# Linear attention and memory attention, four layers: the second multiplier of the queries behind the merge's `kt` loop, the opening's input parts behind the powers, segment 1's moments behind the keys, and a second pause in the preparation of weights

## The chip, the core and the metric

The kernel runs on one core of one Trainium2 chip. The metric is the time of one launch on the device in microseconds, less is better. The core's engines are TensorE (PE: matrix products and transposes, with weight loads counted apart as PEld), VectorE (DVE), ScalarE (ACT), GpSimd (POOL) and SyncE (SP). Each works through its own row of instructions in order; an instruction that waits holds up everything behind it on its engine. DMA transfers are issued by SP, ACT and POOL from the same rows and run beside the engines.

## The reference

The input x has 2048 rows of 640 numbers. Two kinds of layers, A and B, are applied in turn, A, B, A, B, each to the normalised x, and each adds its result to x.

```
# layer A: linear attention, 32 heads of 20
qkv = layernorm(x) @ wqkv
pq, pk = phi(q), phi(k)             # t + 1 where t > 0, else exp(t); + 1e-6
kv  = einsum("bhsd,bhse->bhde", pk, v);  z = sum over s of pk
o   = (pq @ kv) / (pq . z + 1e-6)
x   = x + o @ wo
# layer B: four segments of 512 rows; in each head
o   = g * (pq @ M) / (pq . z + 1e-6) + (1 - g) * softmax(q k^T / sqrt(20) + mask) @ v
M, z += the segment's phi(k)^T v and sum of phi(k)
x   = x + o @ wo
```

## The kernel before

**Layer A without v.** A layer A never computes v. For every segment of 512 rows (four tiles of 128) it computes the keys' features `pk` (L525 to L536) and the queries' features, which go to DRAM as `pqd` (L542, L543). Then it gathers `G`, the normalised input transposed times `pk`, over the four segments (memory matmuls, L557, added up in the tiles `v` and `g_last`, L562, L564). Only when all segments are in does `merge` form the one matrix that maps queries to results: it broadcasts the sums of `z` (`zb`, L609 to L612), scales `G` and splits it (`gs`, L625 to L628), multiplies with `w_Av` (L642) to block matrices `kt` (L647 to L654, one for each of five blocks of columns), and multiplies these with `w_Ao` to `wm` (L674, L679, L681, L682; "the product"). The queries are then read back a tile at a time by `p_read` (L698): the tile `pqi` is multiplied by `zb` on POOL (L700), summed by head on DVE and inverted (L703 to L705), and multiplied by that on POOL (L706). Then it is transposed on PE (L319) and goes through `wm` (`o_half`, L472).

**Splits.** For precision a weight or an activation is held as the sum of two f16 tensors, so most products are three matmuls. ACT makes the high half, and DVE or POOL the low one: L264 and L265 for weights, L323 and L324 for transposed inputs, L476 (ACT) and L477 (POOL) for the normalised inputs `xs` ("the input parts"), L530 and L531 for the keys, L653 and L654 for `kt`.

**The opening.** While the first layer A runs, the eight weights are prepared (`w_prep`): loaded as f32 into one of two `stage` buffers, reduced to their largest absolute value (L240 five times, L245, a PE transpose at L248, L250, a PE broadcast at L254), scaled by a power of two (L257 to L260), split (L264, L265) and stored to DRAM (`wd`, L270). Layers fetch them again later (L276, on POOL's queue). Normalising an input tile takes the moments (L338 to L345 on DVE, the power -1/2 at L343 on POOL) and one ACT instruction (L368) that makes `xh`; four PE transposes of it make `xT`.

**What sets the order.** The code is made of generators that yield the cost of the matmuls they have just written. `weave` alternates a main generator with a side one: after each step of the main one, two or three steps of the side one (`per`). `pause(n)` yields n empty steps, so it puts n main-side turns, that is their matmuls, between two parts of a side generator. PE's order is the order in which the code was written. The rows of the other engines are set by a scheduler that takes what is ready first by its estimate, and in cases of doubt what was written first. `issue_after(ins)` makes what is written inside it stand behind `ins` on the engine of `ins`. `a_head`, which calls `p_read` for the first three tiles, looks at each turn whether `L["zb"]` is set, and begins when it is. During the merge `filled` puts the last queries' steps between the parts.

Of the kernel before, what the change touches and what calls it, by code (L numbers as in the profile page):

```python
# [21 lines left out]
P = 128  # L22
# [105 lines left out]
def pause(n):  # L128
    for _ in range(n):
        yield 0.0  # L130
# [12 lines left out]
class Kernel:  # L143
# [84 lines left out]
    def w_prep(self, key, stage, w, wait=0, behind=False):  # L228
# [15 lines left out]
        m1 = cp.tile([P, 1], F32, name="wm1", tag="wm1", bufs=2)  # L244
        nc.vector.tensor_reduce(m1, mx, axis=AX.X, op=OP.max)  # L245
        yield 0.0
        pt = self.bank()
        nc.tensor.transpose(pt[:1, :P], m1, self.ident)  # L248
        m2 = cp.tile([1, 1], F32, name="wm2", tag="wm2", bufs=2)
# [83 lines left out]
    def moments(self, x):  # L333

        nc, sb = self.nc, self.sb
        st = sb.tile([P, 2, 6], F32, tag="st", name="st", bufs=3)
        for k in range(2):
            nc.vector.bn_stats(st[:, k], x[:, k * HN:(k + 1) * HN])  # L338
        mv = sb.tile([P, 2], F32, tag="mv", name="mv", bufs=4)
        nc.vector.bn_aggr(mv, st)  # L340
        rs = sb.tile([P, 1], F32, tag="rs", name="rs", bufs=4)
        self.taken = nc.vector.tensor_scalar(rs, mv[:, 1:2], 1e-5, None, op0=OP.add)
        nc.gpsimd.tensor_tensor(rs, rs, self.mhalf, op=OP.pow)  # L343
        nb = sb.tile([P, 1], F32, tag="nb", name="nb", bufs=4)
        self.last = nc.vector.tensor_scalar(nb, mv[:, 0:1], rs, -1.0, op0=OP.mult, op1=OP.mult)  # L345
        return x, nb, rs
# [135 lines left out]

    def norms(self, src, s, box, gap):

        box.append([self.moments(self.load_x(src, s, i)) for i in range(NT)])
        yield from pause(gap)
        yield from self.g_norms(s, box)

# [26 lines left out]
    def g_first(self, s, box, w, L, behind=None):  # L515
# [7 lines left out]
        def keys(i):  # L523
# [3 lines left out]
            for n in range(2):  # L527
                z, c = slice(n * HN, (n + 1) * HN), slice(n * (HN + 1), n * (HN + 1) + HN)
                e = self.phi_a(self.proj_n(xT, w("k"), i, n), self.inv["A", "k"])
                nc.scalar.activation(pk[i][:, 0, c], e, AF.Copy, scale=self.k_scl)  # L530
                nc.vector.scalar_tensor_tensor(pk[i][:, 1, c], e, self.k_scl, pk[i][:, 0, c],  # L531
                                               op0=OP.mult, op1=OP.subtract)
                if s == 0 and i == 0:
                    (nc.gpsimd if L["early"] else nc.vector).tensor_copy(L["z"][:, z], e)
                else:
                    (nc.gpsimd if L["early"] else nc.vector).tensor_tensor(L["z"][:, z], L["z"][:, z], e, op=OP.add)  # L536
                yield self.COST_N
# [50 lines left out]
    def merge(self, L, wv, wo, memory, fill):  # L588
# [26 lines left out]
        for n in range(2):  # L615
# [4 lines left out]
            for c in range(C):  # L620
# [4 lines left out]
                nc.vector.scalar_tensor_tensor(e, L["G"][c][:, n * (HN + 1):n * (HN + 1) + HN], eps[:, c:c + 1],  # L625
                                               rz[:, n * HN:(n + 1) * HN], op0=OP.add, op1=OP.mult)
                nc.scalar.activation(t[:, c, 0, :HN], e, AF.Copy)
                L["split"] = nc.vector.tensor_tensor(t[:, c, 1, :HN], e, t[:, c, 0, :HN], op=OP.subtract)  # L628
        L["zb"] = zb
        for _ in memory:  # L630
            pass
        yield from filled(1)
# [1 line left out]
        for t in range(C):  # L634
# [16 lines left out]
                                           self.blk[:, OFF[t]:OFF[t] + WID[t]].rearrange(h, e=E1)[:, :, :DH],  # L651
                                           op0=OP.mult, op1=OP.mult)
            nc.scalar.activation(k2[:, 0, P:P + hi - lo], e, AF.Copy)  # L653
            nc.vector.tensor_tensor(k2[:, 1, P:P + hi - lo], e, k2[:, 0, P:P + hi - lo], op=OP.subtract)  # L654
            kt.append(k2)
            yield 15 * (hi - lo) * COL
            if t == 1:
                yield from filled(1)
        for v in L["v"]:
            self.ones_column(v)  # L660
        wm = sb.tile([P, C, 2, D], F16, tag="wo", name="wm", bufs=2)
# [405 lines left out]
    def opening(self, src, stage, L, box):  # L1067
# [46 lines left out]
        m = [m]  # L1114
        with self.tc.issue_after(self.last.ins):
            m += [self.moments(x[i]) for i in range(2, NT)]
        def others():
            xh = [first]
            for i in range(1, NT):
                xh.append(self.normed(*m[i - 1]))  # L1120
                yield from self.turn(xh[i], cur[1], i)
            for i in range(NT):
                self.parts(xh[i], cur[2], i)

        o = others()
        self.ones_columns()
# [155 lines left out]
```

## Time and profile before

| | us |
|---|---|
| median of 3 runs | 1739.72 (1735.49 to 1740.57) |
| profiled execution | 1736.56 |
| its span, first to last instruction | 1734.8 |
| mean granted PE clock | 0.992 |
| PE busy | 1651.8 (95%) |
| DVE busy | 1252.2 (72%) |
| ACT busy | 995.6 (57%) |
| POOL busy | 541.1 (31%) |

A row of the time line reads: start in us, duration in us, engine, line, operation, tile written <- tiles read, sizes, xcount (equal instructions in succession are one row), and in brackets how long the engine sat idle before it and what ended that wait. A PE row of many matmuls runs to the start of the next one when there is no bracket. A clock below 1 in the tables means that the matmuls of that stretch ran slower by a throttle. The chain on the page has PE at 70%, DVE at 13%, ACT at 7%: an engine that is busy is not by that on the path.

### The profile page before, as it was taken

To read this page: it belongs to the slowest core of one execution; us is meant where nothing else is said; L and a number is where in the kernel's file an instruction comes from. 1 tells how busy PE (TensorE), PEld (TensorE's weight loads), DVE (VectorE), ACT (ScalarE), POOL (GpSimd) and SP (SyncE) were. 2 spreads that over 40 slices of the span, in tenths; PEclk is the share of its full clock that TensorE was granted. 3 is DMA by queue.
4 is the path that set the end of the run, shared out by engine and by line. 5 is a ranking of instruction groups with operands and counts; after the bars stand their busy time and mean duration, and the time that the engine had idled before them with its cause. 6 is when DMAs were issued, how large, how long until landed. Compare 5 with 4: busy or idle time off the path is not lost.

```text
span 1734.8 us, 36293 instructions
## 1 busy us (share of the span) xinstructions
PE 1651.8 (95%) x13032; PEld 1031.2 (59%) x13032; DVE 1252.2 (72%) x3966; ACT 995.6 (57%) x1883; POOL 541.1 (31%) x1059
## 2 busy tenths in 40 slices
PE   6999989999999999999999999999999999999998
PEld 4677656564465456556566777666546545645555
DVE  7878696387787768768874466846778877878773
ACT  5666433346747646667776554333675576666673
POOL 3542132123213433433452310221422432332452
PEclk9999999999999999999999999999999999999999
DMA  5424563332222331353211303523232323223432
GB/s 214 148 99 147 205 231 125 114 104 70 99 86 60 111 115 65 123 164 112 70 55 39 115 31 115 179 97 121 67 105 83 113 79 110 99 81 112 133 113 92
DMA packets 110365, 190.89 MB, mean 110 GB/s; under 512 B 14172, under 2 KB 69596, under 8 KB 107624
## 3 DMA queue, kind: packets, MB, share of 16 engines
q1 hardware_dynamic: 97704, 142.68, 25.3%
q0 software_dynamic: 3264, 24.91, 4.1%
q10 hardware_dynamic: 9216, 20.98, 3.1%
q8 instruction: 103, 1.69, 0.4%
q14 instruction: 78, 0.64, 0.1%
HBM read 109.32 MB, written 78.64 MB: 108 GB/s over the span
## 4 chain that ended last, share of the span: by engine, by line
PE 70%; DVE 13%; ACT 7%; DMA 4%; issue 3%; POOL 2%; SPq 1%; ACTq 0%; POOLq 0%; DVEq 0%
PE ps L395 28%; PE ps L381 13%; PE ps L993 7%; PE ps L557 4%; PE ps L966 4%; PE ps L925 3%; PE ps L319 3%; ACT pe L970 3%; PE ps L446 2%; DVE ps L931 2%; PE ps L810 2%; PE ps L1006 1%; DVE xn L472 1%; DVE split L265 1%; DVE st L338 1%
## 5 line engine op out<-in xcount | busy, mean ns | idle before, releaser
L931 DVE CUSTOM_DVE_ANT_0 ps<-ps,maskw 128x384 f32<-128x384 f32 (+3 forms) x1024 | 472.9, 519 | 37.2 <-PE ps L925 34.2
L970 ACT ACTIVATE pe<-ps,lsc 128x512 f32<-128x512 f32 x640 | 396.3, 698 | 76.3 <-PE ps L966 74.4
L395 PEld LDWEIGHTS <-xT 128*128 128x128 f16 x2880 | 282.4, 99 | 115.8 <-issue 8.6
L977 POOL TENSOR_SCALAR_AFFINE_SELECT pe<-pe 128x256 f32<-128x256 f32 (+1 forms) x640 | 230.2, 367 | 369.1 <-ACT pe L970 362.4
L395 PEld LDWEIGHTS <-oT 128*128 128x128 f16 x1920 | 184.5, 98 | 81.6 <-issue 5.9
L993 PE MATMUL ps<-pe,v 128*32 128x512 f32 (+3 forms) x2048 | 165.7, 439 | 12.6 <-POOL pe L977 7.3
L931 DVE DVE_READ_ACCUMULATOR2_ANT mg<- 128x1 f32 x1024 | 143.7, 140 | 0.0
L395 PE MATMUL ps<-w_Ak,xT 128*128 128x320 f16 x960 | 141.1, 304 | 2.7 <-ACT w_Ak L264 1.5
L395 PE MATMUL ps<-wm,oT 128*128 128x320 f16 x960 | 141.7, 299 | 2.0
L381 PE MATMUL ps<-xT,w_Bq 128*128 128x512 f16 x600 | 140.3, 379 | 2.8 <-ACT r L419 1.6
L395 PE MATMUL ps<-w_Bo,oT 128*128 128x320 f16 x960 | 141.2, 299 | 1.5 <-ACT oT L323 0.7
L395 PE MATMUL ps<-w_Aq,xT 128*128 128x320 f16 x960 | 140.5, 303 | 1.2 <-DVE xT L324 1.1
L557 PE MATMUL ps<-pk,xs 128*128 128x321 f16 (+1 forms) x960 | 139.0, 302 | 2.1 <-DVE pk L531 1.4
L395 PE MATMUL ps<-w_Bv,xT 128*128 128x320 f16 x960 | 139.7, 299 | 0.6 <-DVE otok L1013 0.6
L381 PE MATMUL ps<-xT,w_Bk 128*128 128x512 f16 x600 | 138.3, 379 | 1.2 <-ACT pe L970 1.2
L925 PE MATMUL ps<-ks,qs 60*128 60x512 f16 (+3 forms) x1024 | 122.9, 298 | 6.8 <-ACT pe L970 3.3
L557 PEld LDWEIGHTS <-xs 128*128 128x128 f16 x960 | 93.6, 98 | 40.6 <-issue 2.1
L775 DVE SCALAR_TENSOR_TENSOR nat<-ps,nat 128x512 f16<-128x512 f32 x80 | 55.2, 690 | 82.9 <-ACT nat L774 82.8
L993 PEld LDWEIGHTS ps<-pe,v 128*32 128x32 f32 x2048 | 65.9, 110 | 74.8 <-issue 39.9
L966 PE MATMUL ps<-qs,ks 62*128 62x512 f16 (+3 forms) x1024 | 106.3, 300 | 2.3 <-ACT pe L970 1.1
L410 DVE SCALAR_TENSOR_TENSOR e<-e,r 128x320 f32<-128x320 f32 x128 | 65.2, 509 | 53.2 <-ACT r L409 52.3
L774 ACT ACTIVATE nat<-ps 128x512 f16<-128x512 f32 x80 | 48.3, 604 | 88.4 <-PE ps L381 69.6
(197 smaller groups left out, 2421.2 us busy)
## 6 DMA issues: line engine op xcount, KB each, us to landing
x<-xn ACTq DMA_DIRECT2D x48, 320.0 KB
qs<-qd SPq DMA_DIRECT2D x128, 120.0 KB
ks<-kd SPq DMA_DIRECT2D x128, 120.0 KB
xo<-x SPq DMA_DIRECT2D x48, 320.0 KB
pqi<-pqd SPq DMA_DIRECT2D x32, 320.0 KB
qd<-nat SPq DMA_DIRECT2D x40, 256.0 KB
kd<-nat SPq DMA_DIRECT2D x40, 256.0 KB
x<-in_A_x SPq DMA_DIRECT2D x16, 320.0 KB
```

Source lines behind the costliest of these rows:

```text
L319: nc.tensor.transpose(pt[:, (c - c0) * P:(c - c0 + 1) * P], src[:, c * P:(c + 1) * P], self.ident)
L381: nc.tensor.matmul(p, w[:, c, a, t * P:(t + 1) * P], xT[:, c, b, :], start=k == 0, stop=k == 3 * C - 1)
L395: nc.tensor.matmul(p, xT[:, c, a, i * P:(i + 1) * P], w[:, c, b, n * HN:(n + 1) * HN], start=k == 0, stop=k == 3 * C - 1)
L410: nc.vector.scalar_tensor_tensor(e, e, 1.0, r, op0=OP.min, op1=OP.add)
L557: nc.tensor.matmul(p, xs[:, i, a, c * P:(c + 1) * P], pk[i][:, b, cols], start=k == 0, stop=k == 3 * NT - 1)
L775: nc.vector.scalar_tensor_tensor(nat[:, 1], p, QK_SHIFT, nat[:, 0], op0=OP.mult, op1=OP.subtract)
L925: nc.tensor.matmul(bs[par][:, a:a + n], qs[r, p, i * P:(i + 1) * P], ks[r, p, :n], start=True, stop=True)
L931: nc.vector.tensor_tensor_reduce(bs[par][:, a:a + n], bs[par][:, a:a + n], self.maskw[:, SEG - n:], 1.0, NEG, OP.add, OP.max, G["mg"][:, p ...
L966: nc.tensor.matmul(b[:, a:a + n], ks[r, p, j * P:(j + 1) * P], qs[r, p, j * P:], start=True, stop=True)
L970: nc.scalar.activation(e, b, AF.Exp, scale=self.lsc)
L977: nc.gpsimd.affine_select(d, d, pattern=pat, compare_op=OP.is_ge, fill=0.0, base=0, channel_multiplier=-1)
L993: nc.tensor.matmul(G["pv"][32 * h4:32 * h4 + 32, j * P:], v[j][:, h * E1:h * E1 + 32], G.pop((p, par, j)), start=j == 0, stop=j == 2, skip ...
```

## The change

Five edits. (1) In `opening`, the input parts of segment 0 (L476, L477) are put behind the last power L343 of segment 0. The mark is a POOL instruction, so it orders POOL's L477 alone. (2) In `norms`, all loads of a segment's input are written first, and for segment 1 the moments are put behind `keyed`, the last split L531 of the keys written so far, which is a DVE instruction. (3) `w_prep` has a second `pause(wait)`, in front of the transpose of the maximum; `wait` is 0 for A's k and q, 3 for A's v and o and for B's v, q and k, and 6 for B's o. (4) In `merge`, `L["zb"]` is set behind the `kt` loop, so that `a_head` begins there. (5) `L["split"]`, behind which `p_read` writes its product L700, becomes the low split of `kt` instead of the low split of `G`.

```
@@ w_prep
         nc.vector.tensor_reduce(m1, mx, axis=AX.X, op=OP.max)
         yield 0.0
+        yield from pause(wait)
         pt = self.bank()
         nc.tensor.transpose(pt[:1, :P], m1, self.ident)
@@ moments
-        nc.gpsimd.tensor_tensor(rs, rs, self.mhalf, op=OP.pow)
+        self.power = nc.gpsimd.tensor_tensor(rs, rs, self.mhalf, op=OP.pow)
@@ norms
-        box.append([self.moments(self.load_x(src, s, i)) for i in range(NT)])
+        x = [self.load_x(src, s, i) for i in range(NT)]
+        with self.tc.issue_after(self.keyed.ins) if s == 1 else nullcontext():
+            box.append([self.moments(t) for t in x])
@@ g_first, keys
-                nc.vector.scalar_tensor_tensor(pk[i][:, 1, c], e, self.k_scl, pk[i][:, 0, c],
+                self.keyed = nc.vector.scalar_tensor_tensor(pk[i][:, 1, c], e, self.k_scl, pk[i][:, 0, c],
@@ merge
-                L["split"] = nc.vector.tensor_tensor(t[:, c, 1, :HN], e, t[:, c, 0, :HN], op=OP.subtract)
-        L["zb"] = zb
+                nc.vector.tensor_tensor(t[:, c, 1, :HN], e, t[:, c, 0, :HN], op=OP.subtract)
...
-            nc.vector.tensor_tensor(k2[:, 1, P:P + hi - lo], e, k2[:, 0, P:P + hi - lo], op=OP.subtract)
+            L["split"] = nc.vector.tensor_tensor(k2[:, 1, P:P + hi - lo], e, k2[:, 0, P:P + hi - lo], op=OP.subtract)
             kt.append(k2)
             yield 15 * (hi - lo) * COL
             if t == 1:
                 yield from filled(1)
+        L["zb"] = zb
@@ opening
+        top = self.power
...
-            for i in range(NT):
-                self.parts(xh[i], cur[2], i)
+            with self.tc.issue_after(top.ins):
+                for i in range(NT):
+                    self.parts(xh[i], cur[2], i)
```

Lines of the changed kernel are 1 higher from L248 and 2 to 3 higher from L486 (L250 is L251, L531 is L534, L654 is L656, L700 is L703, L703 is L706, L706 is L709). In the rows below a row gives line, operation, tile written <- tiles read, size and count.

On DVE near 200 us, at the maximum of `B_wk` (L250, `wm`) and the reductions of `B_wo` (L240, `wmx`), before:

```order
L531 SCALAR_TENSOR_TENSOR pk<-e,k_scl,pk 128x320
L240 TENSOR_REDUCE wmx<-stage 128x1
L410 SCALAR_TENSOR_TENSOR e<-e,r 128x320
L240 TENSOR_REDUCE wmx<-stage 128x1
L542 TENSOR_SCALAR e<-e 128x320
L250 TENSOR_REDUCE wm_2496<-ps 1x1
```

and now:

```order
L545 TENSOR_SCALAR e<-e 128x320
L251 TENSOR_REDUCE wm_2523<-ps 1x1
L411 SCALAR_TENSOR_TENSOR e<-e,r 128x320
L240 TENSOR_REDUCE wmx<-stage 128x1
L534 SCALAR_TENSOR_TENSOR pk<-e,k_scl,pk 128x320
L240 TENSOR_REDUCE wmx<-stage 128x1
```

The maximum of `B_wk` stands ahead of the first reduction of `B_wo` now, and a keys' split behind it.

On DVE in the first merge, at the first block of `kt`, before:

```order
L703 TENSOR_REDUCE rca<-pqi 128x32
L628 TENSOR_TENSOR xT<-ge,xT 128x320 x2
L410 SCALAR_TENSOR_TENSOR e<-e,r 128x320
L704 TENSOR_SCALAR rca<-rca 128x32
L703 TENSOR_REDUCE rca<-pqi 128x32
L542 TENSOR_SCALAR e<-e 128x320
L705 RECIPROCAL rca<-rca 128x32
L704 TENSOR_SCALAR rca<-rca 128x32
L647 MEMSET kt 128x512
L705 RECIPROCAL rca<-rca 128x32
L650 SCALAR_TENSOR_TENSOR ke<-ps,blk 128x140
```

and now:

```order
L649 MEMSET kt 128x512
L631 TENSOR_TENSOR xT<-ge,xT 128x320 x2
L411 SCALAR_TENSOR_TENSOR e<-e,r 128x320
L652 SCALAR_TENSOR_TENSOR ke<-ps,blk 128x140
L545 TENSOR_SCALAR e<-e 128x320
L649 MEMSET kt 128x512
L656 TENSOR_TENSOR kt<-ke,kt 128x140
```

The sums of the queries and their inverses are gone from there. They stand behind the fourth of the ten splits L685 of the product now (L682 before).

On POOL in the second merge, where `w_B...` are the fetches for the next layer, L194 writes the ones into the tiles `v`, and L700 and L706 are the two products on a queries' tile, before:

```order
L700 TENSOR_TENSOR pqi<-pqi,zb 128x640
L194 MEMSET v_83 128x32
L194 MEMSET v_84 128x32
L194 MEMSET v_85 128x32
L194 MEMSET v_86 128x32
L276 DMA w_Bv<-wd_Bv 128x6400
L706 TENSOR_TENSOR pqi<-pqi,rca 128x640
L700 TENSOR_TENSOR pqi<-pqi,zb 128x640 x2
L276 DMA w_Bq<-wd_Bq 128x6400
L706 TENSOR_TENSOR pqi<-pqi,rca 128x640 x2
L276 DMA w_Bk<-wd_Bk 128x6400
```

and now:

```order
L194 MEMSET v_83 128x32
L194 MEMSET v_84 128x32
L194 MEMSET v_85 128x32
L194 MEMSET v_86 128x32
L277 DMA w_Bv<-wd_Bv 128x6400
L277 DMA w_Bq<-wd_Bq 128x6400
L703 TENSOR_TENSOR pqi<-pqi,zb 128x640 x3
L277 DMA w_Bk<-wd_Bk 128x6400
L709 TENSOR_TENSOR pqi<-pqi,rca 128x640 x3
```

All three first products stand behind the fetches of `w_Bv` and `w_Bq`, and all three second products behind that of `w_Bk`. In the first merge the row of POOL now is `w_Bv`, `w_Bq`, the first product three times, the second once, `w_Bk`, the second twice; before, two first products stood at its head and two of the second ones ahead of `w_Bk`, with the third just ahead of it.

Elsewhere: on SP in the first merge the loads of `pqi` stand behind the store of `w_Bo` and six small stores `ks<-one` (L768), where two of them stood ahead of both. On DVE there, the five splits L265 of `w_Bo` stand behind the first splits of `G` instead of ahead of them. In the opening, POOL runs the last two powers and one copy before the first two parts, and ACT has the five high halves of `w_Aq` (L264) ahead of segment 1's first `xh` (L368), where three `xh` stood ahead of them before. PE's own order changes at the weights' transposes and broadcasts alone.

More of the change, by code (lines that the diff above doesn't have):

```diff
@@ L530, in keys @@
                 nc.scalar.activation(pk[i][:, 0, c], e, AF.Copy, scale=self.k_scl)
-                nc.vector.scalar_tensor_tensor(pk[i][:, 1, c], e, self.k_scl, pk[i][:, 0, c],
-                                               op0=OP.mult, op1=OP.subtract)
+                self.keyed = nc.vector.scalar_tensor_tensor(pk[i][:, 1, c], e, self.k_scl, pk[i][:, 0, c],
+                                                            op0=OP.mult, op1=OP.subtract)
                 if s == 0 and i == 0:
```

## The prediction, made before the changed kernel was run

> **What bounds the kernel now.** I read the page's first lines, then the list of waits of TensorE (PE), then the time line of each engine around the longest of these waits, then tables of busy time over two stretches.
>
> ```profile
> span 1734.8 us, 36293 instructions
> PE 1651.8 (95%) x13032; PEld 1031.2 (59%) x13032; DVE 1252.2 (72%) x3966; ACT 995.6 (57%) x1883; POOL 541.1 (31%) x1059
> ```
>
> PE is busy for 1651.8 of 1734.8 us, so all that an edit of order can win lies in 83 us of PE idling, and in stretches in which PE runs at a lower clock after idling.
>
> ```profile
> PE ps L319 <- ACT xh L368: 11.2, 2, 7.6
> PE ps L254 <- DVE wm L250: 4.6, 2, 4.2
> PE ps L674 <- DVE kt L654: 4.4, 2, 3.7
> ```
>
> Columns: total us, number, longest. Of the first, 7.6 us is the kernel's start, which no edit touches; the other 3.6 and the next two rows are the places of the change: the opening, the maximum of `B_wk`, and the merges. The first merge begins near 223 us, the second near 1085 us. Work elsewhere on PE keeps its order.
>
> **Edit 1: the opening's input parts behind the powers.**
>
> ```profile
> 17.84 3.21 POOL L477 TENSOR_TENSOR xs<-xh,xs 128x640 f16<-128x640 f32 x2 [2.83 <-ACT xs L476]
> ```
> ```profile
> 20.00 0.14 DVE L342 TENSOR_SCALAR rs<-mv 128x1 f32<-128x1 f32 x1
> ```
> ```profile
> 23.06 0.90 PE L319 MATMUL ps<-ident,xh 128*128 128x128 f32 x3 [3.60 <-ACT xh L368]
> 23.75 4.21 PE L395 MATMUL ps<-w_Ak,xT 128*128 128x320 f16 x15
> ```
>
> The third input's variance is ready at 20.14, but its power stands behind two parts on POOL until 21.05. With the powers first, 0.9 us of the 3.60 us wait goes. The parts (3.21 us) then run from about 22.5 us; nothing needs them before the memory matmuls at 43 us.
>
> **Edit 2: segment 1's moments behind the last split of segment 0's keys.**
>
> ```profile
> 43.41 0.30 PE L557 MATMUL ps<-pk,xs 128*128 128x321 f16 x1 [0.73 <-ACT pk L530]
> 45.10 0.43 PE L557 MATMUL ps<-pk,xs 128*128 128x321 f16 x2 [1.39 <-DVE pk L531]
> ...
> 45.79 8.35 PE L557 MATMUL ps<-pk,xs 128*128 128x321 f16 x48
> 53.98 0.71 PE L319 MATMUL ps<-ident,xh 128*128 128x128 f32 x5
> ```
> ```profile
> 49.83 3.71 ACT L264 ACTIVATE w_Aq<-stage,scl_Aq 128x640 f16<-128x640 f32 x5 [0.77 <-DVE rs L342]
> ```
>
> Without the moments ahead of them on DVE, the keys come sooner: of 0.73 and 1.39 us I take 1.4, the longer wait; with edit 1, PE comes to the transposes of segment 1 (53.98) at least 1.4 + 0.9 = 2.3 us earlier. But the order on ACT has the normalised first input of segment 1 behind the five `w_Aq` splits now, where three stood ahead of them before. Those splits end at 49.83 + 3.71 = 53.54; they may begin up to 2 us earlier with the earlier keys, and 0.9 us of normalising follows them. So the input is there at about 53.3 and PE waits for it: 0.3 us is kept of 2.3. Ends: -2 (the splits a full 2 us earlier) and +2.5 (splits not earlier, and the clock lost). Term: **-0.3**. Late next: that input.
>
> **Edit 3: one more pause in the weights' preparation.** It moves the transpose of a weight's maximum, and the broadcast behind it, 30 to 37 matmuls back on PE, for A's v and o and B's weights.
>
> ```profile
> 200.64 0.82 DVE L240 TENSOR_REDUCE wmx<-stage 128x1 f32<-128x640 f32 x1 [6.10 <-DMA stage<-in_B_wo]
> ```
> ```profile
> 203.06 0.58 PE L254 MATMUL ps<-wm,ones 1*128 1x1 f32 x2 [4.22 <-DVE wm L250]
> 203.57 7.15 PE L395 MATMUL ps<-w_Aq,xT 128*128 128x320 f16 x30
> ...
> 214.77 4.10 PE L395 MATMUL ps<-w_Ak,xT 128*128 128x320 f16 x29
> ```
>
> Before, L250 of `B_wk` stands on DVE behind a reduction that waits for `B_wo` to land, and PE waits for L250: 4.22 us, and 30 matmuls in 7.15 us where 29 take 4.10 elsewhere, so 2.9 us more by a slow clock. Now L250 stands ahead of that reduction, so the 7.1 us go. But DVE still waits at 200.64 for `B_wo`, now with a keys' split behind it:
>
> ```profile
> 222.44 0.73 DVE L531 SCALAR_TENSOR_TENSOR pk<-e,k_scl,pk 128x320 f16<-128x320 f32 x1 [0.64 <-ACT pk L530]
> ```
> ```profile
> 200.64:223.17 22.53, 20.11 (x126) 13.72 (x126) 19.04 (x38) 13.56 (x27) 7.89 (x11) 0.85 0.43 156
> 223.17:254.65 31.48, 27.88 (x247) 20.47 (x245) 30.53 (x70) 11.18 (x23) 6.65 (x10) 1.00 0.51 191
> ```
>
> (Columns: length, then busy time of PE, weight loads, DVE, ACT, POOL, then clock, DMA share, GB/s.) From that landing to the last keys' split DVE is busy 19.04 of 22.53 us. By the new order three L410, two L542 and one L250 fewer stand in between, about 2.4 us by my estimate from such rows (0.5, 0.3 and 0.3 us each). That leaves 16.6 us of work, and about 1.9 us of waits for ACT at the end (three of 0.64): the last split ends near 219, against 223.17. PE, 7 us earlier, waits for it. Ends: -7.1 (DVE does not bind) and -1 (its slack of 3.5 us not used, and the landing 0.5 to 1.6 us later, because stage buffers come free later). Term: **-4.3**. Late next: DVE, which is full from there on (30.53 of 31.48 us).
>
> **Edit 4: p_read after the `kt` loop.** The product L700 is on POOL and the marked instruction on DVE; the order shows no hold of one on the other. What moves p_read is that `zb` is published later: the loads `pqi`, L700 and the rows L703 to L706 all stand later on SP, POOL and DVE.
>
> ```profile
> 249.93 0.81 DVE L703 TENSOR_REDUCE rca<-pqi 128x32 f32<-128x640 f32 x1
> ...
> 252.90 0.34 DVE L705 RECIPROCAL rca<-rca 128x32 f32<-128x32 f32 x1
> ...
> 254.65 4.01 DVE L654 TENSOR_TENSOR kt<-ke,kt 128x140 f16<-128x140 f32 x1
> ...
> 259.33 0.23 DVE L654 TENSOR_TENSOR kt<-ke,kt 128x140 f16<-128x140 f32 x1
> ```
> ```profile
> 255.72 1.28 POOL L706 TENSOR_TENSOR pqi<-pqi,rca 128x640 f32<-128x640 f32 x1
> 256.95 1.53 POOL L700 TENSOR_TENSOR pqi<-pqi,zb 128x640 f32<-128x640 f32 x1
> ...
> 271.89 0.58 POOL L276 DMA_DIRECT2D w_Bk<-wd_Bk  x1 [4.70 <-PE ps L679]
> ```
> ```profile
> 258.71 0.45 PE L674 MATMUL ps<-w_Ak,kt 128*128 128x320 f16 x1 [3.67 <-DVE kt L654]
> 259.27 0.98 PE L679 MATMUL ps<-w_Ak,kt 128*32 128x320 f16 x3
> ...
> 264.48 0.58 PE L679 MATMUL ps<-w_Ak,kt 128*32 128x320 f16 x6
> ...
> 271.52 1.09 PE L319 MATMUL ps<-ident,pqi 128*128 128x128 f32 x8
> 272.65 2.53 PE L395 MATMUL ps<-wm,oT 128*128 128x320 f16 x15
> ```
>
> First merge. Ahead of the first `kt` split, two each of L703, L704 and L705 leave DVE: 2 x (0.81 + 0.34) = 2.3, and with the two small L704 between them I take 2.5 off the chain. The split took 4.01 us against 0.23 while POOL ran L706 and L700, and PE waited 3.67 us. With POOL's products behind it this goes, but three L700 now run back to back (4.6 us) and can hold a later split; PE then has groups of the product in hand. I take half: 1.9. Behind that wait five groups run at 0.98 us, where later ones take 0.58: 5 x 0.4 = 2 us of slow clock, of which half again, 1.0. Against that, POOL's `w_Bk` fetch waits for the last L679, and the second and third L706 stand behind it, where before they stood ahead: 0.58 + 1.28 us after the last L679 for PE's eight transposes, 0.4 us for the wake-ups between them by my estimate, and some for loads that land late, in all 2.5. Sum: -2.5 - 1.9 - 1.0 + 2.5 = **-2.9**. Ends: -7.4 (everything but 1.5 kept) and +2 (a split still held, the transposes 5 us late).
>
> The SBUF page of the Trainium skill ("SBUF — State Buffer", "Who interferes with whom") says that VectorE and GpSimd share one port pair, that the first to start holds it for its whole instruction, and that the other is blocked until then. Taken by the letter a `kt` split would wait for one product, 1.5 us, and the term would be 1 us better; the row of 4.01 us spans the whole of one L706 and one L700 with a fetch before them, so the train counts, and the sum goes by the row.
>
> Second merge:
>
> ```profile
> 1100.71 0.31 PE L674 MATMUL ps<-w_Ak,kt 128*128 128x320 f16 x1 [0.74 <-DVE kt L654]
> ...
> 1108.23 0.31 PE L679 MATMUL ps<-w_Ak,kt 128*32 128x320 f16 x1 [2.19 <-DVE kt L654]
> 1108.47 0.58 PE L674 MATMUL ps<-w_Ak,kt 128*128 128x320 f16 x3
> ```
>
> These 2.9 us go, as L703 leaves the `kt` chain. But now all three L706 stand behind `w_Bk`, so behind the last L679: 0.4 + 0.58 + 2 x 1.28 = 3.5 us of lateness, less 0.1 that overlap. Term: **+0.5**, ends -1.5 (only one product late) and +3.5 (the loads behind the fetches as well).
>
> **Sum.** -0.3 - 4.3 - 2.9 + 0.5 = -7.0. The profiled execution took 1736.56 us, so 1729.6 for one like it. It lies 3.2 us under the median of the three runs, 1739.72, whose own spread is 5 us; a median of the changed kernel should be about 1739.72 - 7.0 = 1732.7.
>
> **The rivals.** What a measurement tells from no change here is about 0.3%, 5.2 us: under 1734.5 is faster, over 1744.9 slower.
>
> A, the backlog keeps it. DVE is full from 200 to 255 us, and if the landing of `B_wo` is later by 1.6 us and the `w_Bo` splits sit in DVE's chain, edit 3 gives -1 and edit 4 its -2.9: with the others -3.7, 1736.0. For it: 30.53 of 31.48 us. Against it: the wait of 6.10 us on DVE shows that work can be put ahead.
>
> B, slower: the loads of `pqi` become the end of both merges.
>
> ```profile
> 216.01 1.40 SPq L698 DMA_DIRECT2D pqi<-pqd  x2
> ...
> 239.33 4.55 SPq L768 DMA_DIRECT2D ks<-one  x6
> ```
> ```profile
> w_Bv<-wd_Bv POOLq DMA_DIRECT2D x1, 1600.0 KB, 9.0
> ```
>
> Before, two of the first three loads were issued at 216.01; now all four stand behind the `w_Bo` store and six `ks` issues (4.55 us), beside fetches of 1600 KB that take 9.0 us. Issued at 249 (my estimate: 4.55 us and a store behind the `w_Bo` splits) and landing 8 us later, three L700 (4.6), L703 to L705 (2.5), one L706, the fetch and two more L706 (4.4 together) bring the transposes to 268.5 instead of 271.52. That is -3.0 for the edits up to there, whatever they won before it, +3.5 in the second merge, +0.5 together: 1740.2. Each us that the loads land later counts twice, so from a landing 10.4 us after the issue it is slower by over 0.3%; at 11 us, 1746. Against it: 320 KB are a fifth of such a fetch.
>
> C, the change doesn't do what it says: no edge holds L700 on POOL, so it falls on a `kt` split as before. Edit 4 then gives -2.5 + 2.5 = 0, the whole -4.1: 1735.6.
>
> D, all is kept: -2 - 7.1 - 7.4 - 1.5 = -18, 1721.7.
>
> What the new waits of 2 to 3 us do to the clock is open. The row at 45.10 (0.73 and 1.39 us of idling, then 48 matmuls in 8.35 us, 0.174 each, against 4.10 / 29 = 0.141) says 1.6 us for each; the group at 1108.47 runs at full speed (0.58 us) behind 2.19 us of idling, which says nothing. I take nothing, and put 1.6 us each into the upper ends. The Trainium skill ("TensorE: Matmul & The Clock Gate", Part 1) lets the clock fall after an idle window of about 3.4 us: by that the new waits cost nothing, as the second row has it, and the first row disagrees.
>
> **Chances.** Forecast 0.45 (own range 1727 to 1735, the four ends taken by a third), A 0.14, B 0.24, C 0.10, D 0.07. Faster are D and nearly all of the forecast (0.48 after its upper edge); A, C and that edge lie within 0.3%, 0.28; B, taken with its later landings, is the slower side, 0.24. The range takes in most of B and half the way to D: 1724 to 1746.
>
> **What would show it.** Right: no wait of PE at L254 near 203 us; the last keys' split near 219; the first `kt` split at about 0.23 us; a wait at the `pqi` transposes of 1 to 3 us in both merges, with the `w_Bk` fetch ahead of it on POOL; a wait for segment 1's first input near 50 us. Wrong, if PE waits over 5 us at those transposes, if the last keys' split is still at 222, or if the opening at 64 us is off by over 2 us.

## The result and the profile after

The changed kernel takes 1730.60 us (median of 5 runs, 1728.51 to 1732.77) against 1738.55 us (median of 5, 1735.49 to 1740.57) of the kernel before. The ratio is 0.9954, with a 95% interval of 0.9938 to 0.9970: 8.0 us less, where 7.0 less had been forecast. (The 1739.72 of the forecast was the median of the first three of these five runs of before.) The profiled execution took 1731.61 us, its span is 1729.8 us, so 5.0 less than before: the pair of profiles shows 3 us less of a gain than the medians do. The page's first lines and rows of PE's list of waits:

```profile
span 1729.8 us, 36293 instructions
PE 1649.9 (95%) x13032; PEld 1032.5 (60%) x13032; DVE 1249.1 (72%) x3966; ACT 997.0 (58%) x1883; POOL 539.3 (31%) x1059
```
```profile
PE ps L320 <- ACT xh L369: 12.0, 3, 7.7
PE ps L320 <- POOL pqi L709: 9.3, 4, 7.2
...
PE ps L255 <- DVE wm L251: 1.2, 2, 0.9
```

The waits for `kt` (4.4 us for its first rows) and for the maximum of `B_wk` (4.2) are gone from the head of the list, and a wait of 9.3 us for `pqi` has come, 7.2 of it at one place. The time line of PE shows the first merge first:

```profile
215.88 3.74 PE L560 MATMUL ps<-pk,xs 128*128 128x321 f16 x24
220.67 1.31 PE L612 MATMUL ps<-z,square 128*128 128x320 f32 x4 [1.06 <-DVE square L608]
...
249.53 0.57 PE L677 MATMUL ps<-w_Ak,kt 128*128 128x320 f16 x3
...
259.97 0.58 PE L682 MATMUL ps<-w_Ak,kt 128*32 128x320 f16 x3
260.97 0.77 PE L320 MATMUL ps<-ident,pqi 128*128 128x128 f32 x5 [0.42 <-POOL pqi L709]
262.80 0.55 PE L320 MATMUL ps<-ident,pqi 128*128 128x128 f32 x3 [1.06 <-POOL pqi L709]
263.18 2.42 PE L396 MATMUL ps<-wm,oT 128*128 128x320 f16 x15
```

and then the second:

```profile
1090.38 0.57 PE L677 MATMUL ps<-w_Ak,kt 128*128 128x320 f16 x3
...
1100.13 0.58 PE L682 MATMUL ps<-w_Ak,kt 128*32 128x320 f16 x3
1107.95 2.14 PE L320 MATMUL ps<-ident,pqi 128*128 128x128 f32 x8 [7.24 <-POOL pqi L709]
1109.88 3.61 PE L396 MATMUL ps<-wm,oT 128*128 128x320 f16 x15
1113.33 0.38 PE L320 MATMUL ps<-ident,pqi 128*128 128x128 f32 x2
```

The first merge's product runs with no wait of any size and at full clock, and pays 1.5 us at the transposes of `pqi`. The second merge's product runs through too, but then PE waits 7.24 us, and afterwards its transposes take 2.14 us and its 15 matmuls 3.61, where both merges of before have 1.09 and 2.53: the clock had fallen (0.63 in a table further down). DVE and POOL in the first merge, with the last keys' split, the first and the third split of `kt`, and the three first products:

```profile
218.70 0.72 DVE L534 SCALAR_TENSOR_TENSOR pk<-e,k_scl,pk 128x320 f16<-128x320 f32 x1 [0.64 <-ACT pk L533]
...
247.52 0.23 DVE L656 TENSOR_TENSOR kt<-ke,kt 128x140 f16<-128x140 f32 x1
...
252.37 0.62 DVE L656 TENSOR_TENSOR kt<-ke,kt 128x160 f16<-128x160 f32 x1 [2.31 <-ACT kt L655]
```
```profile
251.28 4.67 POOL L703 TENSOR_TENSOR pqi<-pqi,zb 128x640 f32<-128x640 f32 x3 [0.22 <-DMA pqi<-pqd]
```

To set one execution against another I use the starts of five rows of PE in each profile: the queries of segment 0 (its first L395 after 60 us), the memory matmuls of segment 3 (the first L557 after 205 us), the first product in the first merge (L674), its first output, and, in the second merge, from its first `w_Av` matmul to the second 15 matmuls of its first output. All entries are us, from such rows, one profile each.

| profile | start to queries, segment 0 | to memory, segment 3 | to first product | to first output | second merge | span |
|---|---|---|---|---|---|---|
| before | 64.34 | 158.56 | 31.69 | 18.06 | 24.55 | 1734.8 |
| after | 66.07 | 149.81 | 33.65 | 13.65 | 29.93 | 1729.8 |
| after less before | +1.73 | -8.75 | +1.96 | -4.41 | +5.38 | -5.0 |

The first four stages lie end to end and come to -9.5 at the first output. The stretches not in the table take off 0.9 more.

### The profile page after: what moved, and what is told of

The parts are those of the page before. It is cut to its first block, busy times and chain, and to the rows that moved or that the text cites. A ratio compares the mean times of both kernels' runs of the same rounds, so it can differ in the third digit from the quotient of the medians.

```text
span 1729.8 us, 36293 instructions
## 1 busy us (share of the span) xinstructions
PE 1649.9 (95%) x13032; PEld 1032.5 (60%) x13032; DVE 1249.1 (72%) x3966; ACT 997.0 (58%) x1883; POOL 539.3 (31%) x1059
## 4 chain that ended last, share of the span: by engine, by line
PE 73%; DVE 12%; ACT 7%; POOL 3%; issue 2%; DMA 2%; SPq 0%; ACTq 0%; POOLq 0%; DVEq 0%
PE ps L396 31%; PE ps L382 13%; PE ps L996 7%; PE ps L560 5%; PE ps L320 4%; PE ps L969 4%; PE ps L928 3%; ACT pe L973 3%; DVE ps L934 2%; PE ps L447 2%; PE ps L813 2%; PE ps L1009 1%; DVE wmx L240 1%; DMA pqi<-pqd 1%; PE ps L805 1%
```

## The experiments

### Where the change's time comes from: edit 3 alone, edits 1 to 3, edits 4 and 5

Edit 3 alone is the kernel before with one line more (the names `power`, `keyed` and `top` are set too and not used):

```
         yield 0.0
+        yield from pause(wait)
         pt = self.bank()
```

> The second pause in w_prep alone. The sum on record has -4.3 for it; the profiles so far say that PE gets 8.5 us at the memory matmuls of the last segment and gives about 2 back in the first merge. Theory T5 (this edit alone is the change's whole gain): no wait near 203 us, PE 8 to 9 us nearer to the memory matmuls of segment 3 from the queries of segment 0 than before, a kt split of 2 to 4 us in the first merge, the second merge as before, median 5 to 7 us under the kernel before. Rival R5 (edits 1 and 2 are needed for it): 3 us or less.

Measured: 1731.16 us (5 runs) against 1736.89 of before beside it, ratio 0.9965 (0.9952 to 0.9978), 5.7 us less. From the queries of segment 0 to the memory matmuls of segment 3 it takes 149.80 us, 8.8 less than before, and PE has no wait near 203 us. The held `kt` split takes 2.46 us. T5 holds, but for the second merge: it takes 25.92 us, not 24.55 as before, because three groups of its product run at 0.98 us behind a wait of 2.23 us.

The second kernel has edits 1, 2 and 3, and leaves `zb` and the mark at their old places; against the changed kernel:

```
@@ merge, behind the splits of G
+                L["split"] = nc.vector.tensor_tensor(t[:, c, 1, :HN], e, t[:, c, 0, :HN], op=OP.subtract)
+        L["zb"] = zb
         for _ in memory:
...
@@ merge, behind the kt loop
-        L["zb"] = zb
```

> Edits 1 to 3 alone; zb is published where it was before. By the sum on record these three give -0.3 - 4.3 = -4.6 us. Theory T3 (the prediction's): no wait near 203 us, the last keys' split about 4 us earlier, DVE full behind it, the kt split of 4 us and the waits at 250 to 259 us of before still there, the second merge as before; median 3 to 5 us under the kernel before. Rival R3 (without the late p_read the earlier arrival is worth nothing, since the splits wait in the first merge anyway): median within 1.5 us of the kernel before.

Measured: 1731.11 us (10 runs) against 1736.94, ratio 0.9970 (0.9959 to 0.9982), 5.8 us less. Its profile has the first product of the merge at 247.60 and the first output at 265.17, 17.57 us later, about as before (18.06): a split is still held (2.88 us, and PE waits 2.55 us for it). The second merge takes 24.44 us, as before. What T3 says of the waits holds; the last keys' split comes 6.5 us earlier, not 4, and the gain is above the 3 to 5 us that it gave. R3 falls: the earlier arrival is worth its time without the late p_read.

The third kernel has edits 4 and 5 alone; against the changed kernel:

```
@@ w_prep
-        yield from pause(wait)
@@ norms
-        x = [self.load_x(src, s, i) for i in range(NT)]
-        with self.tc.issue_after(self.keyed.ins) if s == 1 else nullcontext():
-            box.append([self.moments(t) for t in x])
+        box.append([self.moments(self.load_x(src, s, i)) for i in range(NT)])
@@ opening
-            with self.tc.issue_after(top.ins):
-                for i in range(NT):
-                    self.parts(xh[i], cur[2], i)
+            for i in range(NT):
+                self.parts(xh[i], cur[2], i)
```

> Edits 4 and 5 alone. By the sum on record they give -2.9 in the first merge and +0.5 in the second. Theory T4 (the second merge is the wrong term, +4.4 instead of +0.5, and the first merge was about right): the wait near 203 us as before (4.2 us), the first product of the first merge about 3 to 6 us earlier than before against the same place at 223 us, a wait of over 6 us at the pqi transposes of the second merge, median between 1.5 us under and 2 us over the kernel before. Rival R4 (the loads land late only because the first three edits brought the merge forward): the wait at the second merge stays under 4 us and the median is 2 to 5 us under the kernel before.

Measured: 1739.34 us (10 runs) against 1736.94, ratio 1.0012 (1.0003 to 1.0021), so 2.4 us more, a little over what T4 gave. Its first product lies 29.56 us behind the memory matmuls of segment 3 instead of 31.69, so 2.1 us nearer, where T4 gave 3 to 6. On PE, DVE and POOL of this kernel:

```profile
201.67 0.58 PE L254 MATMUL ps<-wm,ones 1*128 1x1 f32 x2 [4.36 <-DVE wm L250]
...
257.60 0.31 PE L679 MATMUL ps<-w_Ak,kt 128*32 128x320 f16 x1 [3.67 <-DVE kt L653]
...
1113.65 2.14 PE L319 MATMUL ps<-ident,pqi 128*128 128x128 f32 x8 [6.52 <-POOL pqi L706]
```
```profile
253.46 4.08 DVE L653 TENSOR_TENSOR kt<-ke,kt 128x160 f16<-128x160 f32 x1 [0.93 <-ACT kt L652]
```
```profile
252.84 4.51 POOL L700 TENSOR_TENSOR pqi<-pqi,zb 128x640 f32<-128x640 f32 x3
```

R4 falls: the second merge's wait of 6.5 us comes without the first three edits. What I had as a risk in the prediction, the three L700 in a row holding a later split, is here: the third block's split, issued during the first of them, ends with the last of them, 4.08 us later, and PE waits 3.67 us, as long as before the change. So edits 4 and 5 alone move the held split from the first block to the third and pay for the second merge on top. From the memory matmuls of segment 3 to the first output it takes 48.20 us (221.06 to 269.26) against 49.75 before: 1.5 us won there, and some 5 us lost in the second merge.

In the first merge the edits help each other. From the memory matmuls of segment 3 to the first output before takes 49.75, edits 1 to 3 take 51.45, edits 4 and 5 take 48.20, and all five 47.30, 2.6 less than the two differences add up to (49.90). These are single profiles; two more kernels, which leave the first merge as it is in the changed one, take 47.00 and 47.41.

The time in all is another matter. Edit 3 gives 5.7 us, edits 1 to 3 give 5.8, and all five 8.0 in their own comparison, with intervals of 2 to 3 us each way. The 8.0 hangs on that comparison's 1738.55 for the kernel before; against the 1736.30 to 1736.94 of the later ones, 1730.60 is 5.7 to 6.3 us less. So the whole net gain can be edit 3's, and that edits 4 and 5 add to it is not shown. The profiles say why: from edits 1 to 3 to all five, the stretch from the memory matmuls to the first output gets 4.15 us shorter and the second merge 5.49 longer.

### The second merge: when p_read is early there, the loads early, the fetch behind

The first kernel publishes `zb` early in the second merge alone, and moves the mark of edit 5 back there:

```
+        if not L["early"]:
+            L["zb"] = zb
         for _ in memory:
             pass
...
-        L["zb"] = zb
+        if L["early"]:
+            L["zb"] = zb
```

> The changed kernel, but in the second merge zb is published at its old place, so that p_read is late in the first merge alone. Theory T (the second merge costs the change about 4.4 us net, because p_read is late there): PE waits about as before at the second merge (0.7, 0.3 and 2.2 us, a wait of under 0.5 us at the pqi transposes), and the median is about 1726, 4 to 5 us under the changed kernel's 1730.6. Rival R0 (what was lost there is lost for another reason, the earlier arrival colliding with the fetches of the next layer's weights): a wait of over 3 us stays at the pqi transposes, median 1729 to 1731.

Measured: 1726.95 us (4 runs) against 1736.30, ratio 0.9948 (0.9931 to 0.9964). In the profile T holds and R0 falls: the waits in the product are 0.74, 0.25 and 2.35 us, about as before, there is none at the transposes, and the second merge takes 26.23 us instead of 29.93. The time is less clear than T gave it: 1726.95 is 3.65 us under 1730.60, but by the ratios (0.9948 and 0.9954, each against its own runs of before) no difference can be told.

The second kernel leaves p_read late in both, and writes only its first three loads early in the second merge. `L["go"]` is set in `merge` where `zb` was published before, and `p_read` takes its tile from `L["pre"]` while there are any:

```
+    def p_load(self, L, s, i):
+        pq = self.row("pqi")
+        self.q_pqi.dma_start(pq, L["pqd"][s][i])
+        return pq
...
     def a_head(self, L, s, box):
+        if L["zb"] is None and not L["early"]:
+            while not L.get("go"):
+                yield 0.0
+            L["pre"] = []
+            for i in range(3):
+                L["pre"].append(self.p_load(L, s, i))
+                yield 0.0
```

> The changed kernel, but in the second merge the first three loads of pqi are written where zb was published before; the products stay late. Theory T1 (the 7.2 us wait at the pqi transposes comes from the loads landing late, beside two fetches): the first products on POOL start at the merge's beginning or at once when written, the wait falls to 2 to 3.5 us, the clock stays up, median about 1726. Rival R1 (it comes from the row of POOL, where the second products stand behind the fetch of w_Bk): the wait stays over 5 us, median about 1730.

Measured: 1721.24 us (4 runs, 1718.87 to 1721.55) against 1736.30, ratio 0.9911 (0.9896 to 0.9926). The whole wait is gone, which is more than T1 gave. The scheduler moves the first products on POOL with the loads: they start at 1069.18, 1082.45 and 1086.09 us, two of them ahead of both fetches. SP of the changed kernel, then of this one:

```profile
1064.13 26.32 SPq L546 DMA_DIRECT2D pqd<-e  x4
1090.62 2.16 SPq L701 DMA_DIRECT2D pqi<-pqd  x4
```
```profile
1041.29 22.73 SPq L546 DMA_DIRECT2D pqd<-e  x6
1064.12 1.50 SPq L700 DMA_DIRECT2D pqi<-pqd  x3
1085.80 4.13 SPq L546 DMA_DIRECT2D pqd<-e  x2
```

POOL of the changed kernel, and the DMA engines' share there (the last three columns are clock, DMA share and GB/s):

```profile
1087.94 0.53 POOL L277 DMA_DIRECT2D w_Bv<-wd_Bv  x1 [2.95 <-PE ps L396]
1090.84 0.53 POOL L277 DMA_DIRECT2D w_Bq<-wd_Bq  x1 [2.37 <-PE ps L644]
1100.12 1.53 POOL L703 TENSOR_TENSOR pqi<-pqi,zb 128x640 f32<-128x640 f32 x1 [8.76 <-DMA pqi<-pqd]
1102.35 3.02 POOL L703 TENSOR_TENSOR pqi<-pqi,zb 128x640 f32<-128x640 f32 x2 [0.70 <-DMA pqi<-pqd]
1105.31 0.59 POOL L277 DMA_DIRECT2D w_Bk<-wd_Bk  x1
1106.64 3.72 POOL L709 TENSOR_TENSOR pqi<-pqi,rca 128x640 f32<-128x640 f32 x3 [0.73 <-DVE rca L707]
```
```profile
1090.00:1100.00 10.00, 10.00 (x84) 4.39 (x81) 5.74 (x16) 4.44 (x12) 0.53 (x1) 1.00 0.96 392
1100.00:1110.00 10.00, 2.76 (x14) 1.89 (x13) 5.30 (x13) 1.41 (x4) 8.44 (x7) 0.63 0.68 246
```

SP's row is held by the last four stores of the queries until 1090.45, and behind them stand all four loads. They go out between two fetches of 1600 KB, the DMA engines are busy for 96% of the next 10 us, and the first load has landed only when POOL can begin at 1100.12, 9.5 us after its issue. With the loads ahead of the last two stores the second merge takes 20.83 us instead of 29.93, and 24.55 before the change. PE goes straight from the product into the transposes:

```profile
1097.75 0.58 PE L683 MATMUL ps<-w_Ak,kt 128*32 128x320 f16 x3
1098.26 1.09 PE L320 MATMUL ps<-ident,pqi 128*128 128x128 f32 x8
1099.39 2.53 PE L396 MATMUL ps<-wm,oT 128*128 128x320 f16 x15
```

The third kernel is the changed one with the fetch of `w_Bk` put behind the third L709 on POOL:

```
@@ p_read
-        nc.gpsimd.tensor_tensor(q3, q3, rc[:, :, None].to_broadcast([P, H, DH]), op=OP.mult)
+        x = nc.gpsimd.tensor_tensor(q3, q3, rc[:, :, None].to_broadcast([P, H, DH]), op=OP.mult)
+        if i == 2:
+            self.third = x
@@ dense
-                    wB["k"] = self.fetch(("B", "k"))
+                    with self.tc.issue_after(self.third.ins):
+                        wB["k"] = self.fetch(("B", "k"))
```

> The changed kernel, but the fetch of w_Bk stands behind the third second product L709 on POOL in both merges. Theory T1 (the loads land late): in the second merge the wait of 7.2 us falls by 0.6 us at most, in the first merge the waits of 0.4 and 1.1 us fall to about 0.5 together; median 1729 to 1730. Rival R1 (the fetch of w_Bk holds the products): the second merge's wait falls under 4 us, median about 1726.

Measured: 1729.72 us (7 runs) against 1736.30, ratio 0.9971 (0.9960 to 0.9982). The wait at the second merge is 6.32 us instead of 7.24, so R1 falls; it is shorter by a little more than T1's 0.6. In the first merge the second of the two waits goes from 1.06 to 0.46 us: there the fetch does stand in the way, by its own 0.6 us. But PE then waits about as long for the next thing, DVE's split of the transposed tile:

```profile
260.06 1.94 PE L396 MATMUL ps<-wm,oT 128*128 128x320 f16 x13 [0.64 <-DVE oT L325]
```

From the end of the product to the second 15 matmuls it takes 5.21 us here and 5.10 in the changed kernel, so nothing is won in the first merge. Lateness of the loads is the cause in the second merge: POOL waits 8.76 us for them there, and the wait goes when they come early. The place of the fetch is a small addition at most.

### The opening: without edit 2

This kernel takes back the `norms` part of the change:

```
-        x = [self.load_x(src, s, i) for i in range(NT)]
-        with self.tc.issue_after(self.keyed.ins) if s == 1 else nullcontext():
-            box.append([self.moments(t) for t in x])
+        box.append([self.moments(self.load_x(src, s, i)) for i in range(NT)])
```

> The changed kernel without edit 2 (segment 1's moments where they were before). Theory T2 (the opening lost 1.7 us because segment 1's first normalised input now comes behind the five splits of w_Aq): no wait at segment 1's first transposes, PE at the queries of segment 0 (66.1 us in the changed kernel) about 1.7 to 2.5 us earlier, and, as DVE holds the first merge up from 201 us on, at most half of it is left at the end: median 1729 to 1730. Rival R2 (the opening lost it by edit 1, the parts on POOL at 22 to 26 us): the wait of 2.0 us at those transposes goes, but PE is no earlier at the queries of segment 0.

Measured: 1729.91 us (5 runs, 1727.34 to 1732.14) against 1736.30, ratio 0.9961 (0.9948 to 0.9974); the changed kernel's own ratio is 0.9954, so no difference can be told. No wait is left at segment 1's first transposes, and PE is at the queries of segment 0 at 62.91, 3.2 us earlier, where T2 gave 1.7 to 2.5, so R2 falls. ACT and DVE of the changed kernel show where that wait comes from:

```profile
46.76 3.71 ACT L265 ACTIVATE w_Aq<-stage,scl_Aq 128x640 f16<-128x640 f32 x5 [2.95 <-DVE scl_Aq L261]
54.35 0.92 ACT L369 ACTIVATE xh<-x,nb,rs 128x640 f32<-128x640 f32 x1 [3.88 <-DVE nb L346]
```
```profile
48.96 4.01 DVE L266 SCALAR_TENSOR_TENSOR w_Aq<-stage,scl_Aq,w_Aq 128x640 f16<-128x640 f32 x5
...
53.30 0.14 DVE L343 TENSOR_SCALAR rs<-mv 128x1 f32<-128x1 f32 x1
```
```profile
55.33 0.77 PE L320 MATMUL ps<-ident,xh 128*128 128x128 f32 x5 [2.00 <-ACT xh L369]
```

ACT has its splits of `w_Aq` done at 50.47 and then waits 3.88 us. On DVE the five low splits (4.01 us) stand ahead of L343 at 53.30, from which POOL's power and DVE's `nb` (L346) follow at once. So T2 has the mechanism right, an input that comes too late, and the engine wrong. But the size of the loss, 1.7 us, is partly chance: kernels with the same opening as the changed one have their queries of segment 0 at 63.92, 63.98, 64.13, 64.50 and 65.55 us in the other runs' profiles, and kernels without edit 2 at 62.87 to 65.24. The waits vary less. The one for segment 1's first input is 2.00 to 2.29 us in all six profiles with edit 2, and there is none in the seven without. The one for DVE's splits of the keys is 0.84 to 0.93 us with edit 2 and 1.26 to 1.40 without. So edit 2 wins 0.5 us at the keys and loses 2 at that input. The wait for ACT's half of the keys, 0.30 to 2.49 us, varies with edit 2 and without, and so does the clock: the 48 memory matmuls after the waits at 43 us take 6.75 us in one and 7.87 in another run of the same instructions (clock 1.00 and 0.85 over them):

```profile
45.46 7.87 PE L560 MATMUL ps<-pk,xs 128*128 128x321 f16 x48
```

for the changed kernel, and for the one with the fetch behind, whose opening is the same:

```profile
44.23 6.75 PE L560 MATMUL ps<-pk,xs 128*128 128x321 f16 x48
```

### Versions that are better than both

Four kernels combine what helped, each by the edits shown above. The first is the one with early loads in the second merge, less edit 2.

> The changed kernel with the second merge's loads early (as in the run before) and without edit 2. Theory (the two losses are separate, 9 us in the second merge and 2 to 4 us in the opening): the first product of the first merge about 4 us earlier than in the changed kernel, no wait at the pqi transposes of the second merge, median 1717 to 1719. Rival (what the opening gives is lost again, as the median without edit 2 was only 0.7 us under the changed kernel's): median about 1721.

Measured: 1722.97 us (4 runs, 1718.62 to 1726.12), ratio 0.9925 (0.9908 to 0.9941): the rival's side; edit 2 is not a loss of 2 us. The second writes the loads early in both merges:

```
-        if L["zb"] is None and not L["early"]:
+        if L["zb"] is None and True:
```

> As the run before it, with the loads early in the first merge too. Theory: the waits of 0.9 and 1.1 us at the first merge's pqi transposes go, up to 2 us more, median 1715.5 to 1718. Rival (DVE's sums then stand in the kt chain again, as one of the three does by the order, and hold it up): no better or up to 2 us worse than the run before it.

Measured: 1722.61 us (4 runs), ratio 0.9917 (0.9903 to 0.9932), no better. The waits at the first merge's transposes (0.46 and 1.07 us in the run before it) go, as the theory says, but one sum (L703 in the kernel before) stands among the first `kt` splits again. From the memory matmuls of segment 3 to the first output it takes 46.94 us against 46.74 of the run before it: what one gives, the other takes.

The third has early loads in the second merge and the fetch of `w_Bk` behind, with edit 2.

> The changed kernel with the second merge's loads early and the fetch of w_Bk behind the third second product. Theory (the waits of 0.4 and 1.1 us at the first merge's transposes are due to that fetch): the first merge 1 to 2 us shorter than in the run with early loads alone, the second as there (20.8 us from its first product to the second half of the first output), median 1719 to 1721. Rival (they are due to the sums on DVE): as the run with early loads alone, 1721.2.

Measured: 1720.30 us (4 runs, 1718.61 to 1723.12) against 1736.89, ratio 0.9907 (0.9892 to 0.9922). The second merge takes 20.83 us again. In the first merge the second wait is 0.46 us, but as above 0.65 us of waiting for DVE follow it: the theory's 1 to 2 us are not there. The median is where the theory had it, but it also lies within the spread of the runs with early loads alone (1718.87 to 1721.55). And the same without edit 2:

> The run before it without edit 2. Theory (edit 2 costs about 1 us in the opening, whose clock varies by as much from run to run): PE at the queries of segment 0 at 62.9 to 64.6 us, median within 1.5 us of the run before it. Rival (edit 2 is worth its place): 2 us or more slower than the run before it.

Measured: 1721.95 us (4 runs, 1718.88 to 1724.89), ratio 0.9909 (0.9892 to 0.9925). Its queries of segment 0 are at 65.24 in the profile, outside the theory's 62.9 to 64.6, its median 1.65 above the run before, where 1.5 was given: neither reading can be told from the runs' spread (1718.88 to 1724.89). The best version is thus 1720 to 1721 us, about 16 us or 0.9% under the kernel before and 10 under the changed one, and the 0.9 us between it and early loads alone is not resolved.

One edit needs no run: with edit 5 undone, the program of the changed kernel is the same, instruction for instruction, on all five engines. The mark on DVE does not order POOL's products, as the prediction had read from the order, so "edits 4 and 5" is edit 4.

## Why the prediction was right

The sign and the size came out right (forecast 1732.7, measured 1730.6, within the range of 1724 to 1746). But the size is luck in good part: two errors of 4 to 5 us, one each way, made the sum good. And one of the prediction's own signs of being wrong came true, a wait of over 5 us at the transposes of `pqi`. Of its other signs, no wait near 203 us, the first `kt` split at 0.23 us and a wait of 1.5 us in the first merge were there. (The prediction's edit 4 is edits 4 and 5 of the list.)

**Opening, -0.3.** Measured +1.73 in the profile, and -0.4 to +1.7 over six profiles with this opening against the one profile of before. By the means of these six and of the three profiles without edits 1 and 2 (64.34, 62.87, 63.24) it is +1.2: a small loss where a small gain was forecast, inside the term's ends. The input of segment 1 is late, as said, and not by ACT's splits but by DVE's. The 1.4 us that the keys were to win came to 0.5, by DVE's splits of the keys. Edit 1's 0.9 is borne out: the wait for the third input is 3.09 to 3.60 us in three profiles without it and 2.10 to 2.74 in ten with it.

**Edit 3, -4.3, and the first 2.5 of edit 4.** Taken together, the stretch from the queries of segment 0 to the first product is 190.25 us before and 183.46 after: -6.8, the very sum of the two terms. That is luck too, since the terms do not add: over this stretch edit 3 alone gives 6.7 and edits 4 and 5 alone 2.5. Edit 3's term was too small, and with edit 3 in place the 2.5 gives almost nothing more there. The last keys' split ends at 219.42, where "near 219" was forecast, but with the queries of segment 0 1.73 us later; counted from them it came 5.5 us nearer, not 4.2. DVE binds behind it, as said (waits of 1.06 and 0.86 us): PE gains more than the 7.1 up to the memory matmuls (8.75) and gives 1.96 back.

**The rest of edit 4 in the first merge.** -1.9 and -1.0 had been taken as halves, +2.5 for the transposes. Measured -4.41 from first product to first output: the 3.67 us wait and the 2 us of slow clock went whole, and the transposes cost 1.5, not 2.5. The split held by three L700 in a row was a real risk, shown by the run of edits 4 and 5 alone; in the changed kernel the splits took 0.62, 0.48 and 0.96 us beside the three L703. Why DVE came in between here and not there is open.

**Second merge, +0.5: this step failed.** It took 5.38 us more. The step priced L706 behind the `w_Bk` fetch (3.5 us) and left the loads to rival B. Measured, the 3.2 us of waits in the product went as said (from first product to the end of the product 10.3 us instead of 14.1), but the loads land 9.5 us after an issue at 1090.62, and their wait costs 7.24 us plus about 1.9 us of slow clock. That is rival B's mechanism with its landing time nearly right (8 us after the issue taken, 9.5 measured), in one merge and not in both: in the first merge the loads go out at 245.65 us and the first product runs at 251.28, 5.6 us later, early enough. POOL's wait of 8.76 us for the loads and the run with early loads show it. The sum hid it: +4.9 lost here, and 4.0 won in the rest of edit 4.

**Rivals.** A falls: edit 3 gave its time. C's premise is true, since no edge holds the product on POOL; its consequence, a held split, falls for the changed kernel and comes true in the run of edits 4 and 5 alone. D had the size of what is there if the loads come early: 16 us.

## What to carry to other kernels

When a step is moved later to take it out of the way, split it into its load and its work, and move only the work: here the load's lateness went with the fetches beside it when it went out, and with the stores ahead of it on its queue. A wait that another instruction on the same in-order engine passes on (here the maximum of one weight behind the landing of the next) is worth moving before anything is rearranged in the busy stage behind it. When an edit's terms are measured, measure them alone and together: here two that were to add up covered for each other. When terms of a sum go both ways, look at each in its own stage; a right sum can hide a loss of 5 us and a further gain of 10.

## What was not expected of the hardware

What short waits do to the clock differs between executions of the same rows. The 48 memory matmuls in the opening take 8.35 us (clock 0.80) behind waits of 0.73 and 1.39 us in the kernel before, and 6.75 us (clock 1.00) behind waits of 1.36 and 1.39 in the run of edits 4 and 5, whose opening is the same. In the run with `zb` early in the second merge, 2.35 us of waiting is followed by a group at full speed and one of 0.91 us, and then, 1.6 us after the wait, by three at 0.98 us:

```profile
1095.99 0.31 PE L687 MATMUL ps<-w_Ak,kt 128*32 128x320 f16 x1 [2.35 <-DVE kt L660]
...
1097.59 0.98 PE L682 MATMUL ps<-w_Ak,kt 128*128 128x320 f16 x3
```

With edit 3 alone, 2.23 us at the same place is followed at once by three such groups. In the kernel before 2.19 us cost nothing there, and with edits 1 to 3 2.08 us. The Trainium skill ("TensorE: Matmul & The Clock Gate", Part 1) has a window of about 3.4 us that runs freely, so that the point of the change moves from run to run; the openings that differ by 1.1 us with the same instructions agree with that, and a fall after 2.35 us does not agree with its idle window taken by the letter. So a price of 0 to 2 us for such a wait is about what can be said beforehand, and it makes most of the spread of up to 8.5 us between runs of one kernel here, by my reading; that was not tested.

A DVE instruction of some 0.3 us was held 4.08 us by three POOL products of 1.5 us each, so through a train and not through one instruction, while in the changed kernel the like of it took 0.48 to 0.96 us beside the same three. The Trainium skill ("SBUF — State Buffer", "Who interferes with whom") describes a block for the whole of one instruction; the runs show holds shorter than one product and a hold of three.
